# One Trainium2 core, attention and two expert layers: split steps asked for one by one, weight sums on Pool, decoding moved to the second batch

## The chip, the core and the metric

The program runs on one core of a Trainium2 chip. A time is the device time of one execution in microseconds. PE is the matrix engine, PEld its weight load, DVE the vector engine, ACT the scalar engine, POOL the GpSimd engine, and SP the engine whose queue issues every DMA of this kernel.

## What is computed

```python
# attention with decay: 2 batches, 8 heads, 768 steps, 64 wide
state = gamma * state + k_t v_t^T ;  y_t = scale * q_t state
# x: 1536 x 512. eight experts, every row through every expert, weighted by a balanced gate P
for e in range(8):
    h = np.maximum(x @ w1[e], 0.0)          # 512 -> 1024
    out += P[:, e:e + 1] * (h @ w2[e])      # 1024 -> 512
# last layer, 512 -> 2048 -> 512
h = x @ w_in
g = np.maximum(h, 0.0) + alpha * np.minimum(h, 0.0)
return g @ w_out
```

All is float32. `w_in` and `w_out` reach the core as 64-bit numbers and are turned into float32 there ("decoding").

## The kernel before

**Phases.** After the attention come 20 phases. Phases 0 to 7 are the eight experts on the first batch of 768 rows, phases 8 to 15 (`FAST`) the same experts on the second batch, and phases 16 to 19 the last layer, two halves of its 2048 columns for each batch. Each has a first layer (x times w1) and a second layer (h times w2).

**Products.** Every matrix is held as a high part (rounded by ACT) and a low part (what is left, by DVE or Pool), and a product takes three matmuls (`mm3`, L185 to L187). The first layer uses Strassen's scheme: each of four column blocks j has seven products p, so 28 products, in the order of the list `order`: place 0 is (0, 1), place 4 is (0, 7), place 7 is (0, 4), place 11 is (1, 7), place 14 is (1, 4), place 18 is (2, 7), place 21 is (2, 4), place 25 is (3, 7). The seven products of a block share PSUM banks. After product 1 ACT copies bank A to bank B (L687), product 6 adds to B, then DVE forms E = B + d (L690), product 7 adds to B, DVE forms D = B + d (L703; in phases 8 to 15 it writes b at L698), and product 4 adds to B. So PE can't start 6 before ACT's copy, 7 before DVE's E, or 4 before DVE's D.

**Second layers.** In phases 0 to 7 and 16 to 19 the second layer is plain, 6 row tiles of 8 products each; with each tile in two halves there are 12 slots, counted here as places 28 to 39. In phases 8 to 15 it is Strassen's scheme too, 28 units (places 28 to 55), whose right sides `hs` are split by ACT and DVE (L779, L780) and whose w2 pieces (`ws`) come from DRAM.

**Side work.** Four kinds of work ride on the phases, put after products by `at(ph, key, ...)`. (1) The w1 blocks of the next half phase: four adds (`w1_adds`, L113), then three parts a, c, b, each an ACT copy and a subtraction (`w1_part` through `split`, L97 and L98). The adds and lows of two blocks run on Pool, those of the other two on DVE in the second layer. (2) In phases 1 to 7, for the second batch, 32 tiles of w2 are prepared (`prep_load`, `prep_sums`, `prep_low`, `prep_store`): load 512 KB, four adds of 128x256 (L169) and directly behind them the ACT copy (L171), two lows of 128x512 (L175), two stores. Five of them go in each of phases 1 to 6. (3) 32 decodes (`decode_steps`): load, three DVE instructions (`bits`, L583 to L588), one on ACT, two on DVE (`join`, L599 and L602), store and next load. 17 lie in phases 1 to 6, one in phase 7 and 14 in phases 8 to 14. (4) The low parts of w2 (`w2_split`).

**What sets the order.** The schedule is written by hand: each engine's queue holds its instructions in the order in which the Python loop calls them, and an engine never passes over an instruction that waits. SP's queue holds all loads and stores the same way.

Of the kernel before, what the change touches and what calls it, by code (L numbers as in the profile page):

```python
# [44 lines left out]
def tile_kernel(ctx, tc, qkT, kv, ctab, w_gate, w1, w2, w_in, w_out, alpha, out):  # L45
# [235 lines left out]
    with tc.manual_schedule():  # L281
# [630 lines left out]

        xk = []
        for ph in range(len(PHASES)):
# [3 lines left out]
            for j in range(2):  # L918
                m = n + j + 2
                at(ph, (j, 1), lambda m=m: w1_adds(m, pool))  # L920
                at(ph, (j, 2), lambda m=m, eng=eng: w1_part(m, "a", eng))
                at(ph, (j, 7), lambda m=m, eng=eng: w1_part(m, "c", eng))
                at(ph, (j, 3), lambda m=m, eng=eng: w1_part(m, "b", eng))
# [197 lines left out]
```

## Time and profile before

| | us |
|---|---|
| median of 3 runs | 1392.34 (1390.39 to 1392.38) |
| the profiled execution | 1390.61 |
| its span in the profile | 1388.9 |
| PE busy | 1306.0 (94%) |
| DVE busy | 946.9 (68%) |
| ACT busy | 634.6 (46%) |
| Pool busy | 408.6 (29%) |

1.7 us lie outside the span. The page's slices show PE near full nearly everywhere and the granted clock at eight or nine tenths in slices of the first half. An engine's busy time is a sum over stages with different limits, so the stages are read one by one further down.

### The profile page before, as it was taken

What the parts mean: (1) busy time and instruction counts of PE and PEld (TensorE: products, weight loads), DVE (VectorE), ACT (ScalarE), POOL (GpSimd) and SP (SyncE); (2) the same over time, 40 slices, a digit from 0 to 9 for tenths busy, and PEclk for the clock granted to TensorE, in tenths of its full rate; (3) what the DMA queues carried; (4) which work ended last, traced back from release to release, by engine and by line L of the source; (5) the groups of instructions that cost most, each with busy time, mean ns of one, the idle gap of its engine ahead of it and who ended that gap; (6) DMA issues with size and microseconds to landing.
All of it is one profiled execution on the core that took longest, in us unless ns stands there. A gap on an engine that the chain in (4) does not pass through costs nothing.

```text
span 1388.9 us, 19473 instructions
## 1 busy us (share of the span) xinstructions
PE 1306.0 (94%) x7179; PEld 1208.2 (87%) x7179; DVE 946.9 (68%) x1562; ACT 634.6 (46%) x1129; POOL 408.6 (29%) x335
## 2 busy tenths in 40 slices
PE   9899898989797979879999999999999999999998
PEld 6798877778787868868899999999999998989897
DVE  5656676767776767675678786777877676486462
ACT  2553525243433334244546455464644546455360
POOL 4761414141323222230001312203121254426260
PEclk9999999989998999999999999999999999999999
DMA  9563687969696978785586776858577393052211
GB/s 364 174 212 125 198 280 236 315 201 316 216 322 201 319 232 299 252 273 185 195 284 194 271 217 227 297 172 287 183 274 231 112 351 107 31 159 84 77 31 46
DMA packets 152254, 296.80 MB, mean 214 GB/s; under 512 B 11952, under 2 KB 77024, under 8 KB 152160
## 3 DMA queue, kind: packets, MB, share of 16 engines
q1 hardware_dynamic: 152160, 295.57, 64.2%
q8 instruction: 56, 0.92, 0.3%
q14 instruction: 38, 0.31, 0.1%
HBM read 198.24 MB, written 97.28 MB: 213 GB/s over the span
## 4 chain that ended last, share of the span: by engine, by line
PE 66%; DVE 18%; ACT 6%; DMA 5%; issue 3%; SPq 2%; POOL 1%; ACTq 0%; DVEq 0%
PE B L185 8%; PE B L187 7%; PE B L186 7%; PE o L185 5%; PE o L187 5%; PE o L186 5%; PE A L185 4%; PE A L187 4%; PE A L186 4%; DVE pr L169 3%; DVE pr L175 3%; PE E L185 2%; PE E L186 2%; PE E L187 2%; PE D L187 2%
## 5 line engine op out<-in xcount | busy, mean ns | idle before, releaser
L113 POOL TENSOR_TENSOR raw<-raw 128x256 f32<-128x256 f32 x108 | 90.1, 845 | 207.3 <-DMA raw<-in_w_dram 62.5
L780 DVE TENSOR_TENSOR hs<-b,hs 128x768 fp32r<-128x768 f32 x96 | 95.0, 990 | 30.3 <-ACT hs L779 30.3
L690 DVE TENSOR_TENSOR E<-B,d 128x384 f32<-128x384 f32 x80 | 45.0, 563 | 80.8 <-PE B L187 75.5
L171 ACT ACTIVATE pw<-pr 128x1024 fp32r<-128x1024 f32 x32 | 33.9, 1060 | 141.0 <-DVE pr L169 136.0
L779 ACT ACTIVATE hs<-b 128x768 fp32r<-128x768 f32 x96 | 81.0, 844 | 28.9 <-PE B L187 10.7
L812 POOL TENSOR_TENSOR total<-total,t 128x384 f32<-128x384 f32 x56 | 60.0, 1100 | 105.2 <-DVE t L808 105.2
L687 ACT ACTIVATE B<-A 128x384 f32<-128x384 f32 x80 | 38.6, 482 | 87.6 <-PE A L187 85.9
L169 DVE TENSOR_TENSOR pr<-pr 128x256 f32<-128x256 f32 x128 | 65.8, 514 | 3.3
L249 POOL TENSOR_TENSOR xs<-b,xs 128x384 fp32r<-128x384 f32 x6 | 6.1, 1022 | 199.8 <-ACT xs L245 199.8
L187 PE MATMUL B<-hs,ws 128*128 128x384 f32 x192 | 64.2, 334 | 0.0
L185 PE MATMUL B<-hs,ws 128*128 128x384 f32 x192 | 64.2, 334 | 0.0
L186 PE MATMUL B<-hs,ws 128*128 128x384 f32 x192 | 64.2, 334 | 0.0
L175 DVE TENSOR_TENSOR pr<-pr,pw 128x512 fp32r<-128x512 f32 x64 | 48.7, 803 | 16.9 <-ACT pw L171 16.9
L738 DVE SCALAR_TENSOR_TENSOR total<-o,P,total 128x512 f32<-128x512 f32 x42 | 31.3, 746 | 28.9 <-PE o L187 28.9
L703 DVE TENSOR_TENSOR D<-B,d 128x384 f32<-128x384 f32 x48 | 27.0, 563 | 29.6 <-PE B L187 29.4
L113 DVE TENSOR_TENSOR raw<-raw 128x256 f32<-128x256 f32 x84 | 42.2, 519 | 1.4
L185 PE MATMUL A<-hs,ws 128*128 128x384 f32 x128 | 42.9, 335 | 0.0
L186 PE MATMUL A<-hs,ws 128*128 128x384 f32 x128 | 42.9, 335 | 0.0
L187 PE MATMUL A<-hs,ws 128*128 128x384 f32 x128 | 42.8, 335 | 0.0
L732 ACT ACTIVATE total<-o 128x512 f32<-128x512 f32 x18 | 10.8, 598 | 69.3 <-PE o L187 69.3
L645 ACT ACTIVATE hh<-D 128x384 fp32r<-128x384 f32 x32 | 15.7, 490 | 49.3 <-DVE D L703 49.3
L682 ACT ACTIVATE d<-D 128x384 f32<-128x384 f32 x64 | 31.1, 486 | 15.0 <-PE D L187 14.9
(3435 smaller groups left out, 4712.8 us busy)
## 6 DMA issues: line engine op xcount, KB each, us to landing
ws<-c SPq DMA_DIRECT2D x112, 512.0 KB, 5.7
raw<-in_w_dram SPq DMA_DIRECT2D x64, 512.0 KB, 4.7
c<-raw SPq DMA_DIRECT2D x32, 512.0 KB, 5.1
pr<-in_w_dram SPq DMA_DIRECT2D x32, 512.0 KB, 6.7
c<-pw SPq DMA_DIRECT2D x32, 512.0 KB, 5.3
c<-pr SPq DMA_DIRECT2D x32, 512.0 KB, 6.2
raw<-c SPq DMA_DIRECT2D x32, 512.0 KB, 5.4
raw<-wd SPq DMA_DIRECT2D x32, 512.0 KB, 3.6
```

The lines of the kernel that those rows point to most:

```text
L113: eng.tensor_tensor(out=out, in0=in0, in1=in1, op=op)
L169: nc.vector.tensor_tensor(out=out, in0=in0, in1=in1, op=op)
L171: nc.scalar.activation(out=ph2[i], in_=pr[i], func=AF.Copy)
L175: nc.vector.tensor_tensor(out=pr[i][:, a].bitcast(F32R), in0=pr[i][:, a], in1=ph2[i][:, a].bitcast(F32), op=ALU.subtract)
L185: nc.tensor.matmul(ps, ah, bh, start=first, stop=False, skip_group_check=True)
L186: nc.tensor.matmul(ps, ah, bl, start=False, stop=False, skip_group_check=True)
L187: nc.tensor.matmul(ps, alo, bh, start=False, stop=last, skip_group_check=True)
L687: nc.scalar.activation(out=banks[n, "B"], in_=banks[n, "A"], func=AF.Copy)
L690: nc.vector.tensor_tensor(out=banks[n, "E"], in0=banks[n, "B"], in1=banks[n, "d"], op=add)
L779: nc.scalar.activation(out=hi, in_=src, func=AF.Copy)
L780: nc.vector.tensor_tensor(out=lo, in0=src, in1=hi.bitcast(F32), op=ALU.subtract)
L812: nc.gpsimd.tensor_tensor(out=dst, in0=dst, in1=tt[m, h], op=ALU.add)
```

## The change

Every step of the side work gets its own place. `w1_part` falls into `w1_high` (the ACT copy) and `w1_low`, `prep_sums` into two halves and a separate `prep_high`, `hsplit` into `hhigh` and `hlow`. The four adds of the tiles that are prepared in a second layer go to Pool. In phases 1 to 6 the decode in the first layer is gone (12 decodes stay, all in second layers); phase 7 has none; phases 9 to 14 have three each, where they had two, the third in the second layer. A part of the diff (the lines that only rename or renumber are left out):

```diff
-    def w1_part(n, part, eng):
+    def w1_high(n, part):
...
-        hi, lo = split(wp, "w" + part, f"w{part}{n}", src, eng, width)
+        hi, lo = (wp.tile([128, width], F32R, tag=f"w{part}{w}", name=f"w{part}{n}{w}") for w in "hl")
+        nc.scalar.activation(out=hi, in_=src, func=AF.Copy)
+        ws1[n][part] = (lo, src, hi)
...
+    def w1_low(n, part, eng):
...
+        lo, src, hi = ws1[n].pop(part)
+        eng.tensor_tensor(out=lo, in0=src, in1=hi.bitcast(F32), op=ALU.subtract)
         if part == "b":
             w_load(0, n + 2)
...
-    def prep_sums(i):
+    def prep_sums(i, eng, part):
...
-        ):
-            nc.vector.tensor_tensor(out=out, in0=in0, in1=in1, op=op)
+        )[part]:
+            eng.tensor_tensor(out=out, in0=in0, in1=in1, op=op)
+
+    def prep_high(i):
         ph2[i] = pools["prep"].tile([128, 1024], F32R, tag="pw", bufs=2, name=f"pw{i}")
         nc.scalar.activation(out=ph2[i], in_=pr[i], func=AF.Copy)
...
+        def step(ph, pos, *fns):
+            for fn in fns:
+                key = order[pos] if pos < 28 else pos - 28 if ph in FAST else slots[pos - 28]
+                at(ph, key, fn)
...
-        def prep_at(ph, k1, k2, k3):
+        def prep_at(ph, eng, s0, s1, hi, lo, st):
...
-            at(ph, k1, lambda: prep_load(i + 1), lambda: prep_sums(i))
-            hooks.setdefault((ph, k2), []).insert(0, lambda: prep_low(i))
-            at(ph, k3, lambda: prep_store(i))
+            step(ph, s0, lambda: prep_load(i + 1), lambda: prep_sums(i, eng, slice(0, 2)))
+            step(ph, s1, lambda: prep_sums(i, eng, slice(2, 4)))
+            step(ph, hi, lambda: prep_high(i))
+            step(ph, lo, lambda: prep_low(i))
+            step(*(ph, st) if st < 40 else (ph + 1, st - 40), lambda: prep_store(i))
...
+            if 1 <= ph <= 6:
+                for i in (30, 36):
+                    decode_at(ph, i, i + 1, i + 2, i + 3)
+                prep_at(ph, dve, 5, 9, 13, 15, 19)
+                for q in (25, 30, 33, 36):
+                    h = max(q, 27)
+                    prep_at(ph, pool, q, q, h + 2, h + 3, h + 4)
+            elif ph == 7:
+                prep_at(ph, dve, 5, 9, 13, 15, 19)
+                prep_at(ph, dve, 18, 20, 22, 24, 26)
...
-            if 1 <= ph <= 6:
-                if ph > 1:
-                    decode_at(ph, *(order[i] for i in (10, 12, 14, 18)))
-                for i in (2, 8):
-                    decode_at(ph, *(slots[i + q] for q in (0, 1, 2, (4, 3)[i > 2])))
-                prep_at(ph, order[8], order[10], order[12])
-                for i in (0, 3, 6, 9):
-                    prep_at(ph, *slots[i:i + 3])
...
+                elif ph < 2 * E - 1:
+                    decode_at(ph, 4, 6, 7, 8)
+                    decode_at(ph, 12, 14, 15, 17)
+                    decode_at(ph, 40, 42, 43, 46)
```

Three places show what moves. The line numbers of after are higher by 14 to 18 for the same code (L181 are the prepared sums, L142 the w1 lows, L717 is D). The first place is DVE's queue in phase 4, first layer, from E of block 1 (after place 8) to D of block 1 (after place 11). Before:

```order
L690 TENSOR_TENSOR E_3598<-B_3567,d_3581 128x384
L646 SCALAR_TENSOR_TENSOR hl_10_3590<-B_3508,hh_10_3589 128x384
L169 TENSOR_TENSOR pr_3458<-pr_3458 128x256 x4
L646 SCALAR_TENSOR_TENSOR hl_01_3616<-E_3529,hh_01_3615 128x384
L175 TENSOR_TENSOR pr_3458<-pr_3458,pw_3607 128x512 x2
L583 TENSOR_SCALAR ex_0_0_3640<-rd_0_0_3497 128x512
L585 TENSOR_SCALAR a_0_0_3642<-rd_0_0_3497 128x512
L588 SCALAR_TENSOR_TENSOR a_0_0_3642<-rd_0_0_3497,a_0_0_3642 128x512
L703 TENSOR_TENSOR D_3574<-B_3567,d_3581 128x384
```

After:

```order
L181 TENSOR_TENSOR pr_3416<-pr_3416 128x256 x2
L704 TENSOR_TENSOR E_3580<-B_3540,d_3558 128x384
L660 SCALAR_TENSOR_TENSOR hl_10_3572<-B_3484,hh_10_3571 128x384
L181 TENSOR_TENSOR pr_3416<-pr_3416 128x256 x2
L660 SCALAR_TENSOR_TENSOR hl_01_3590<-E_3507,hh_01_3589 128x384
L717 TENSOR_TENSOR D_3551<-B_3540,d_3558 128x384
```

Two of the adds now stand ahead of E; the two lows and the three decode instructions have left the stretch. The lows now stand between E and D of block 2, the decode in the second layer. The second place is Pool's queue from the last w2 low of phase 4 into phase 5 (`raw` are the w1 adds). Before:

```order
L98 TENSOR_TENSOR v18l<-raw_18_3675,v18h 128x1024
L98 TENSOR_TENSOR v19l<-raw_19_3738,v19h 128x1024
L113 TENSOR_TENSOR raw_22_3956<-raw_22_3956 128x256 x4
L98 TENSOR_TENSOR wa22l<-raw_22_3956,wa22h 128x512
L98 TENSOR_TENSOR wc22l<-raw_22_3956,wc22h 128x768
L113 TENSOR_TENSOR raw_23_4055<-raw_23_4055 128x256 x4
```

After:

```order
L98 TENSOR_TENSOR v18l<-raw_18_3644,v18h 128x1024
L98 TENSOR_TENSOR v19l<-raw_19_3706,v19h 128x1024
L181 TENSOR_TENSOR pr_3543<-pr_3543 128x256 x4
L181 TENSOR_TENSOR pr_3808<-pr_3808 128x256 x4
L181 TENSOR_TENSOR pr_3895<-pr_3895 128x256 x4
L181 TENSOR_TENSOR pr_3967<-pr_3967 128x256 x4
L113 TENSOR_TENSOR raw_22_3947<-raw_22_3947 128x256 x4
L142 TENSOR_TENSOR wa22l<-raw_22_3947,wa22h 128x512
L113 TENSOR_TENSOR raw_23_4046<-raw_23_4046 128x256 x4
L142 TENSOR_TENSOR wc22l<-raw_22_3947,wc22h 128x768
```

Sixteen adds stand ahead of the w1 adds, and the second block's adds ahead of the first block's part c. The third place is DVE's queue in phase 10, second layer, behind E of the second half (place 39; `t` are the weighted results). Before:

```order
L841 TENSOR_TENSOR E_10_1_7719<-B_10_1_7633,d_10_1_7675 128x384
L98 TENSOR_TENSOR wc44l<-raw_44_7405,wc44h 128x768
L775 SCALAR_TENSOR_TENSOR hs_10_7733<-b_10_7336,hs_10_7733 128x768
L808 TENSOR_TENSOR t_00_7751<-A_10_0_7594,pb_7297 128x384
L98 TENSOR_TENSOR wb44l<-raw_44_7405,wb44h 128x512
L775 SCALAR_TENSOR_TENSOR hs_11_7760<-b_10_7503,hs_11_7760 128x768
L808 TENSOR_TENSOR t_10_7771<-A_10_1_7604,pb_7297 128x384
```

After:

```order
L859 TENSOR_TENSOR E_10_1_7664<-B_10_1_7578,d_10_1_7620 128x384
L597 TENSOR_SCALAR ex_5_1_7677<-rd_5_1_7442 128x512
L599 TENSOR_SCALAR a_5_1_7679<-rd_5_1_7442 128x512
L602 SCALAR_TENSOR_TENSOR a_5_1_7679<-rd_5_1_7442,a_5_1_7679 128x512
L794 SCALAR_TENSOR_TENSOR hs_10_7682<-b_10_7284,hs_10_7682 128x768
L142 TENSOR_TENSOR wc44l<-raw_44_7350,wc44h 128x768
L826 TENSOR_TENSOR t_00_7701<-A_10_0_7539,pb_7242 128x384
L794 SCALAR_TENSOR_TENSOR hs_11_7707<-b_10_7453,hs_11_7707 128x768
L826 TENSOR_TENSOR t_10_7718<-A_10_1_7549,pb_7242 128x384
L613 SCALAR_TENSOR_TENSOR a_5_1_7679<-a_5_1_7679,ex_5_1_7677 128x512
L616 SCALAR_TENSOR_TENSOR a_5_1_7679<-rd_5_1_7442,a_5_1_7679 128x512
```

The five DVE instructions of a third decode stand in a stretch that had none.

## Rows read from the trace of the kernel before

**Rows 1.** Windows, first layers, phases 1 to 7: length, busy PE, PEld, DVE, ACT, POOL; PEclk.
```profile
129.30:165.20 35.90, 31.71 (x173) 30.83 (x172) 19.28 (x32) 22.85 (x43) 17.02 (x12) 0.95 0.56 179
...
570.10:615.80 45.70, 33.80 (x170) 31.96 (x170) 34.33 (x55) 21.65 (x38) 17.99 (x12) 0.89 0.74 253
sum 291.80, PE 232.45 PEld 223.49 DVE 195.49 ACT 145.74 POOL 116.20; mean PE 33.21 PEld 31.93 DVE 27.93 ACT 20.82 POOL 16.60
```

**Rows 2.** Windows: first layer of phase 16, second of 4, first of 8; then DMA share.
```profile
1132.90:1162.70 29.80, 29.75 (x170) 29.17 (x170) 20.55 (x38) 21.68 (x40) 26.35 (x22) 1.00 0.63 222
388.00:420.50 32.50, 32.50 (x145) 26.89 (x145) 25.39 (x47) 8.49 (x13) 5.14 (x5) 1.00 0.96 313
649.60:685.70 36.10, 32.96 (x185) 32.18 (x184) 21.68 (x33) 19.14 (x36) 0.00 (x0) 0.95 0.64 213
```

**Rows 3.** Windows, phases 9 to 14, sums of six: first layers, then second layers.
```profile
sum 185.80, PE 177.74 PEld 175.80 DVE 130.59 ACT 104.50 POOL 35.56; mean PE 29.62 PEld 29.30 DVE 21.76 ACT 17.42 POOL 5.93
...
sum 173.80, PE 173.80 PEld 173.80 DVE 148.68 ACT 86.20 POOL 42.38; mean PE 28.97 PEld 28.97 DVE 24.78 ACT 14.37 POOL 7.06
```

**Rows 4.** Waits of PE, whole span: waiter, released by: us in total, times, longest.
```profile
PE B L185 <- DVE D L703: 40.3, 8, 5.8
PE B L185 <- ACT B L687: 16.3, 7, 3.8
PE B L185 <- DVE E L690: 13.3, 10, 3.1
```

**Rows 5.** Timeline, phase 4, around place 14: start, us, engine, line, shape [idle before <-releaser].
```profile
359.77 3.34 POOL L113 TENSOR_TENSOR raw<-raw 128x256 f32<-128x256 f32 x4
361.22 2.63 DVE L169 TENSOR_TENSOR pr<-pr 128x256 f32<-128x256 f32 x4
...
365.88 2.35 DVE L175 TENSOR_TENSOR pr<-pr,pw 128x512 fp32r<-128x512 f32 x2
...
368.15 1.48 DVE L583 TENSOR_SCALAR ex<-rd 128x512 uint32<-128x512 uint32 x1
...
370.61 0.56 DVE L703 TENSOR_TENSOR D<-B,d 128x384 f32<-128x384 f32 x1
...
371.23 0.69 PE L185 MATMUL B<-xh,wb17h 128*128 128x384 f32 x1 [5.83 <-DVE D L703]
```

**Rows 6.** Timeline, end of phase 4 and start of phase 5.
```profile
421.64 1.79 DVE L169 TENSOR_TENSOR pr<-pr 128x256 f32<-128x256 f32 x4
...
423.51 1.06 ACT L171 ACTIVATE pw<-pr 128x1024 fp32r<-128x1024 f32 x1 [2.70 <-DVE pr L169]
...
425.00 0.44 PE L185 MATMUL B<-xh,wc20h 128*128 128x384 f32 x1 [2.29 <-ACT B L687]
```

**Rows 7.** Groups of instructions: count, then busy us, mean ns, idle us before.
```profile
L113 POOL TENSOR_TENSOR raw<-raw 128x256 f32<-128x256 f32 x108 | 90.1, 845 | 207.3 <-DMA raw<-in_w_dram 62.5 <-DVE raw L113 55.1 <-DMA raw<-wd 39.1
...
L169 DVE TENSOR_TENSOR pr<-pr 128x256 f32<-128x256 f32 x128 | 65.8, 514 | 3.3
L175 DVE TENSOR_TENSOR pr<-pr,pw 128x512 fp32r<-128x512 f32 x64 | 48.7, 803 | 16.9 <-ACT pw L171 16.9
...
L599 DVE SCALAR_TENSOR_TENSOR a<-a,ex 128x512 f32<-128x512 f32 x32 | 25.2, 787 | 1.0 <-DVE a L588 0.5
```

**Rows 8.** Window of the whole span, instructions on tile rd alone: DVE busy.
```profile
0.00:1388.90 1388.90, 74.94 (x128) 0.98 0.64 214
```

**Rows 9.** Timeline of DVE, phase 4, between D of block 1 and D of block 2.
```profile
373.81 1.61 DVE L98 TENSOR_TENSOR v16l<-raw,v16h 128x1024 fp32r<-128x1024 f32 x1 [1.52 <-ACT v16h L97]
...
379.73 0.56 DVE L703 TENSOR_TENSOR D<-B,d 128x384 f32<-128x384 f32 x1
```

**Rows 10.** Timeline of DVE, phase 10, second layer, near its end.
```profile
828.35 1.77 DVE L780 TENSOR_TENSOR hs<-b,hs 128x768 fp32r<-128x768 f32 x1
830.04 0.54 DVE L805 TENSOR_TENSOR t<-B,d 128x384 f32<-128x384 f32 x1
```

**Rows 11.** DMA issues: size, median us from issue to landing.
```profile
pr<-in_w_dram SPq DMA_DIRECT2D x32, 512.0 KB, 6.7
```

More of the change, by code (lines that the diff above doesn't have):

```diff
@@ L917, in tile_kernel @@
             eng = dve if fast else pool
[L918 to L923, printed above, removed]
-            if not fast:
+            if 1 <= ph <= 6:
[8 more added lines that the diff above has]
+                prep_at(ph, dve, 18, 20, 22, 24, 26)
+            if fast:
+                w1_at(ph, n + 2, pool, dve, 0, 2, 3, 3, 5, 7, 9)
+                w1_at(ph, n + 3, pool, dve, 5, 9, 10, 10, 12, 14, 16)
+                w1_at(ph, n + 4, pool, dve, 36, 36, 38, 39, 41, 42, 44)
+                w1_at(ph, n + 5, pool, dve, 44, 44, 46, 47, 49, 50, 52)
+            else:
+                w1_at(ph, n + 2, pool, pool, 0, 3, 3, 6, 6, 9, 9)
+                w1_at(ph, n + 3, pool, pool, 5, 10, 10, 12, 12, 16, 16)
+                if ph > 0:
+                    w1_at(ph, n + 4, dve, dve, 29, 29, 30, 31, 32, 31, 32)
+                    w1_at(ph, n + 5, dve, dve, 33, 33, 34, 35, 36, 35, 36)
                 for j, key in enumerate(((2, 1), (2, 2), (3, 1), (2, 3))):
@@ L967, in tile_kernel @@
-                for key, jp in ((5, 0), (7, 1)):
-                    at(ph, key, lambda ph=ph, jp=jp: t4(ph, jp))
+                        step(ph, (1, 4, 6, 8)[q // 2], lambda m=q // 2, h=q % 2: gather(m, h))
+                step(ph, 0, lambda ph=ph: weight_load(ph))
+                for pos, fn, jp in ((17, t1, 0), (20, t2, 0), (24, t3, 0), (27, t1, 1), (29, t2, 1), (31, t3, 1)):
+                    step(ph, pos, lambda ph=ph, fn=fn, jp=jp: fn(ph, jp))
+                highs = (11, 25, 18, 28, 21, 30, 32, 34, 36, 38, 40, 42, 44, 46)
@@ L969, in tile_kernel @@
+                lows = (13, 26, 19, 28, 23, 30, 32, 34, 36, 38, 40, 42, 44, 46)
+                for k in range(14):
+                    step(ph, highs[k], lambda ph=ph, k=k: hhigh(ph, k))
+                    step(ph, lows[k], lambda ph=ph, k=k: hlow(ph, k))
+                for pos, jp in ((33, 0), (35, 1)):
+                    step(ph, pos, lambda ph=ph, jp=jp: t4(ph, jp))
                 if ph in (E + 1, E + 4):
-                    at(ph, (0, 1), lambda k=(ph - E - 1) // 3: xk.extend(x_keep(2, k)))
+                    step(ph, 0, lambda k=(ph - E - 1) // 3: xk.extend(x_keep(2, k)))
@@ L971, in tile_kernel @@
                 if E < ph < 2 * E - 1:
-                    for keys in (((2, 1), (2, 2), (2, 7), (3, 4)), (9, 11, 13, 17), (18, 20, 22, 27)):
+                    for keys in ((12, 17, 18, 27), (37, 39, 41, 45), (46, 48, 50, 55)):
                         i = unit[0] - NJ * E
@@ L976, in tile_kernel @@
                         unit[0] += 1
-                        for q, key in enumerate(keys):
-                            at(ph, key, lambda i=i, q=q: xk[i][q]())
+                        for q, pos in enumerate(keys):
+                            step(ph, pos, lambda i=i, q=q: xk[i][q]())
             if ph + 1 in XGROUP:
@@ L1040, in tile_kernel @@
             for t in range(TT):
[L1041 to L1042 removed]
+                do(ph, f"t{t}a")
                 do(ph, f"t{t}")
```

77 lines of the change are left out of this document (31 added, 46 removed).

## The prediction

> **What bounds the kernel now.** I read the windows by stage first, then PE's waits, then the timelines around the longest of them. Phase 16 shows what a first layer takes when nothing is late: 29.8 us, PE busy for 29.75 of them, granted clock 1.00 [rows 2]. The same 28 products take 291.8 us in the seven phases 1 to 7 [rows 1], where 7 x 29.8 = 208.6 would do: 83.2 us over. PE's busy sum there is 232.45, so 59.3 us are idle, and the other 24 are matmuls at a lower clock (0.95 in phase 1, 0.89 in phase 7). The second layers have nothing to give: PE is busy for 32.50 of 32.50 us [rows 2]. Phase 8 is 36.1 - 29.8 = 6.3 over [rows 2], and the first layers of phases 9 to 14 are 185.8 - 6 x 29.8 = 7.0 over [rows 3]. So 83.2 + 6.3 + 7.0 = 96.5 us is all that side work can give back.
>
> Who ends these waits: DVE's D 40.3 us in 8 waits, ACT's copy to B 16.3 in 7, DVE's E 13.3 in 10 [rows 4]. The reader should see queues here, not slow engines. Before the D that frees product 4 of block 1, DVE works off the adds of a w2 tile (2.63 us, stretched beside Pool's adds), its lows (2.35) and three decode instructions (the first 1.48); D comes at 370.61, PE has been idle for 5.83 us, and its next matmul shows 0.69 us [rows 5]: the clock has fallen to the lower of its two levels, 1.2 GHz. At a phase's start ACT's copy of a w2 tile waits 2.70 us for DVE's adds, the copy to B stands behind it, and PE is idle for 2.29 us [rows 6].
>
> **The change part by part.** A product takes 29.8/28 = 1.06 us, a second-layer slot 32.5/12 = 2.71 us [rows 2].
>
> The wait at place 14. PE gives DVE five products, 5.3 us, from the end of product 6 (place 8) to the start of product 4 (place 14). DVE now has E, two hl and D in that stretch, taken at D's 0.56 each [rows 5], and two adds, 1.0 us at the mean of 0.514 [rows 7] or 1.3 at the pace of rows 5: 3.3 to 3.6 us. It fits, so the 5.8 us and the fall of the clock go.
>
> What is late next: D of block 2, behind the lows that came there. D to D took 379.73 - 370.61 = 9.12 us [rows 5, 9], 1.52 of it a wait for ACT. A decode costs DVE 74.94/32 = 2.34 us on its loaded tile [rows 8] and 0.79 for the fifth instruction [rows 7], 3.13 together; its two last, some 1.4, leave this stretch and two lows, 1.6 us at the mean [rows 7], 2.35 at worst [rows 5], come in: 9.3 to 10.1, with D itself 9.9 to 10.6. PE gives nine products, 9.6 us. I expect a wait of 0.4 us a phase; the bounds are below 0 (the 1.52 us can take up the lows) and 1.0.
>
> The wait at the phase's start. `prep_high` stands two slots, 5.4 us, behind Pool's four adds, 3.4 us at 0.845 [rows 7]; ACT need not wait for them, and the 16.3 us of rows 4 go. The last low of a phase stands just ahead of the next phase's E. DVE's second layer is 25.39 us busy [rows 2]; without 16 adds of 0.514, 8.2 us, it is 17.2. Pool's 16 adds are 13.5 us. If every one of them held DVE for its whole length, DVE would need 30.7 of 32.5 us. So it ends in time on the whole; I put 0.5 us on its lateness at the end (0 to 1.5) and 0.6 on waits that today's longer ones hide. That is 1.5 us of waits a phase, 31.3 us for a first layer, none long enough for the clock to fall. In phase 7 a second tile stays on DVE in the first layer, four adds and two lows, 2.1 + 1.6 = 3.7 us more late in it: 3.0 us of waits (1.5 to 5.2), 32.8. Together 6 x 31.3 + 32.8 = 220.6, and 291.8 - 220.6 = **71.2 us gained**.
>
> Pool itself: the adds are 0.845 us here against 0.514 on DVE, 1.64 times [rows 7]. The Trainium skill ("GPSIMD Engine Reference", Engine selection) speaks against the move: two-input elementwise work belongs on VectorE, GpSimd being about two times slower; the trace agrees in direction, and by its factor of two the 16 adds would be 16.4 us instead of 13.5, which Pool also has room for. Pool is busy for 5.14 us of the second layer [rows 2] and 16.6 of the first [rows 1]; with 13.5 it has 18.6 of 32.5. Behind its new adds stand the w1 adds and lows of the next phase, and ACT's w1 copies and PE wait for those. The cover: a tile's load lands 6.7 us after issue [rows 11], three slots are 8.1, and PE first uses these weights at place 12, 12.7 us into the phase. If the cover goes, each us of lateness is a us of PE.
>
> SP's queue holds the same loads and stores; a tile's stores come about one slot later, and a store that waits for its low holds the loads behind it. The DMA share is 0.96 in the second layer [rows 2] and keeps its four tiles and two decodes; the first layer (0.56 to 0.74 [rows 1]) loses a decode but is shorter. I cost it at nothing, with the load's 6.7 us as cover.
>
> Phases 9 to 14. The first layers' 7.0 us of waits behind DVE's E go: the w1 copies are asked for before the ACT work that they stood behind. The third decode goes into second layers where DVE is busy for 24.78 of 28.97 us [rows 3]; 3.13 more make 27.9. In phase 10 the add at 830.04 ends at 830.58 [rows 10], and unit 25, product 4 of the second half, starts at 806.1 + 25 x 1.036 = 832.0: 1.4 us to spare against 3.1, so up to 1.7 us late. Less if DVE is less held by Pool, as in the 1.77 us split of rows 10. I take 0.7 a phase, 4.2, and net **2.8 gained** (between 7.0 - 10.2 = -3.2 and 7.0).
>
> Phase 8 keeps its decodes; its last w1 copy is asked for two products earlier, so that loads and stores behind it leave earlier: **2.0 gained** of 6.3 (0 to 6.3). Phases 0 and 16 to 19 only change slots where PE is already full: nothing, within 1.
>
> Sum: 71.2 + 2.8 + 2.0 = 76.0, and 1390.6 - 76.0 = 1314.6. The profiled execution lay 0.2 us above the fastest and 1.7 below the median, so the forecast is **1315 us**, its own range 1302 to 1325.
>
> **The rivals.** A: Pool's adds hold DVE. For it: DVE's four adds took 2.63 us beside Pool's [rows 5] and 1.79 elsewhere [rows 6]. Pool now adds all through the second layer, so DVE enters the next phase late, or the lows meet Pool's w1 lows, and PE waits some 3 us a phase in one go. Rows 6 show 2.29 us with the clock down after it; the lower clock costs 24.2/7 = 3.5 us a phase now, for two falls, so 1.75 for one. 4.75 instead of 1.5 is 3.25 more, times 7 is 23: 1338. Against it: the 30.7 of 32.5 above. The Trainium skill ("SBUF — State Buffer", Who interferes with whom) states the rule behind it: a DVE instruction with two SBUF inputs and a GpSimd instruction that reads SBUF exclude each other, and the later one blocks fully until the other ends. The stretched adds of rows 5 agree.
>
> B: the second batch gives back more. All of the 1.7 us in six second layers (10.2 instead of 4.2), and the second decode, whose load is now asked for four products before its use instead of seven, 4.2 us where loads of its size take 6.7 [rows 11], holds E of block 2 and eats the 7.0: 6 + 7 = 13, 1328. For it: DVE is the fullest engine beside PE there. Against it: PE has two products to spare at that E.
>
> C, slower than before: Pool becomes the bound of phases 1 to 7. Its work there is 16.6 + 5.1 + 13.5 = 35.2 us, a phase is 41.7 + 32.5 = 74.2 now. From 2.1 times today's pace on, under the exclusion from DVE, the phases grow; at 2.3 times it is 81 us, 6.8 x 7 = 48 more: 1438. Against it: the 0.845 us of rows 7 already stand beside a busy DVE.
>
> D: the waits only move, to D of block 2 or E, and no time changes: 1388 to 1393. It needs 10 us of new waits a phase, where DVE has 27.93 - 3.13 = 24.8 us of work in a first layer of 29.8.
>
> E: no wait is left: 1390.6 - 96.5 = 1294, up to 1301.
>
> **How the numbers follow.** Chances: forecast 0.55, A 0.20, B 0.14, E 0.06, C 0.03, D 0.02. The range from 1300 to 1342 takes in forecast, A and B and leaves out E, C, D and the tails. About 0.2% is what a measurement of this kernel can tell from no change; faster by more holds for all but C and D: 0.95, same 0.02, slower 0.03.
>
> **What would show it.** Right: no wait for ACT's copy to B over 1 us in phases 1 to 7, no wait for D at place 14, granted clock 1.00 throughout these phases, first layers of 30 to 32 us, second layers still 32.5 with DVE at some 20 to 25 us and Pool at 18 or more. For A: a wait for E at place 4 or D at place 21 of 2 us and more, with a lower clock behind it. For B: second layers of phases 9 to 14 over 29.0 us with a PE wait for DVE's t. For C: PE waiting at places 12 to 19 for Pool's w1 lows. The forecast is wrong if the first layers of phases 2 to 6 stay above 35 us.

## The result, and the profile after

The changed kernel took 1338.04 us (median of four runs, 1336.02 to 1340.08) against 1391.37 of the kernel before in the same comparison; the ratio is 0.962, 95% interval 0.9598 to 0.9642. It is faster, and inside the stated range of 1300 to 1342; but it lies outside the forecast's own range of 1302 to 1325, 23 us above the forecast of 1315. The profiled execution took 1338.82 us with a span of 1336.8, 52.1 less than before.

Windows of the changed kernel, columns as in [rows 1] (PEclk and DMA share near the end): the sum of the first layers of phases 1 to 7, the second layer of phase 4, the first layer of 8, and of phases 9 to 14 the sums of first and of second layers.

```profile
sum 224.80, PE 210.31 PEld 204.44 DVE 165.78 ACT 133.33 POOL 130.25; mean PE 30.04 PEld 29.21 DVE 23.68 ACT 19.05 POOL 18.61
...
353.00:385.50 32.50, 32.50 (x145) 26.91 (x144) 25.21 (x37) 9.62 (x13) 17.55 (x18) 1.00 0.92 310
...
581.30:619.40 38.10, 33.52 (x185) 32.55 (x184) 21.94 (x33) 18.92 (x37) 0.00 (x0) 0.91 0.64 209
...
sum 192.30, PE 182.00 PEld 178.76 DVE 141.57 ACT 105.60 POOL 44.39; mean PE 30.33 PEld 29.79 DVE 23.59 ACT 17.60 POOL 7.40
...
sum 181.50, PE 176.04 PEld 173.58 DVE 164.69 ACT 89.54 POOL 34.38; mean PE 29.34 PEld 28.93 DVE 27.45 ACT 14.92 POOL 5.73
```

| stage | before | after | change | predicted |
|---|---|---|---|---|
| first layers, phases 1 to 7 | 291.8 [rows 1] | 224.8 | -67.0 | -71.2 |
| first layer, phase 8 | 36.1 [rows 2] | 38.1 | +2.0 | -2.0 |
| first layers, phases 9 to 14 | 185.8 [rows 3] | 192.3 | +6.5 | -7.0 |
| second layers, phases 9 to 14 | 173.8 [rows 3] | 181.5 | +7.7 | +4.2 |
| before phase 0 | 63.74 | 62.37 | -1.4 | 0 |

The sum is -52.2. The other stages moved by half a us or less, phases 16 to 19 taken together; within them single stages moved by up to 1.8 us either way (the first layer of phase 18 took 31.5 us instead of 29.7, with a wait of 1.6 for D, the second layer of phase 17 32.8 instead of 34.5). The attention before phase 0 has the same code and took 62.4 to 65.0 in the runs below, so that row is scatter. PE's waits in the changed kernel, as in [rows 4]:

```profile
PE B L199 <- DVE D L717: 11.2, 9, 1.6
PE B L199 <- DVE E L704: 10.5, 11, 4.1
PE B L199 <- DVE b L712: 9.1, 7, 2.0
PE B L199 <- DVE t L823: 4.8, 4, 1.2
...
PE B L199 <- ACT B L701: 0.8, 4, 0.2
```

The long D waits and ACT's copy to B are gone. Two lines are new: b (product 7 of phases 8 to 15) and t (the result add of their second layers).

**What is left in phases 1 to 7**: some 2.0 us a phase, as in phase 4. DVE's timeline there (start, us, engine, line, shape, idle before), with PE's late product 4 of block 2:

```profile
331.73 2.93 DVE L181 TENSOR_TENSOR pr<-pr 128x256 f32<-128x256 f32 x2
...
335.05 0.55 DVE L717 TENSOR_TENSOR D<-B,d 128x384 f32<-128x384 f32 x1
...
338.25 2.03 DVE L98 TENSOR_TENSOR v16l<-raw,v16h 128x1024 fp32r<-128x1024 f32 x1 [1.53 <-ACT v16h L97]
340.20 0.55 DVE L704 TENSOR_TENSOR E<-B,d 128x384 f32<-128x384 f32 x1
340.81 0.44 PE L199 MATMUL B<-xh,wc18h 128*128 128x384 f32 x1 [0.71 <-DVE E L704]
...
341.13 2.22 DVE L189 TENSOR_TENSOR pr<-pr,pw 128x512 fp32r<-128x512 f32 x2
...
345.48 0.45 PE L199 MATMUL B<-xh,wb18h 128*128 128x384 f32 x1 [1.28 <-DVE D L717]
```

The two adds ahead of D took 2.93 us, beside Pool's w1 lows, which follow one another from 331.10 to 335.8. So D of block 1 came 1.2 us after PE had finished product 7 (place 11, at 333.8). PE had enough in hand there, but the delay runs on through ACT, whose copies stand behind that D and for which DVE then waits 1.53 us, into E and D of block 2, where PE waits 0.71 and 1.28 us.

**Phase 9**, first layer: DVE and Pool ahead of b, and PE behind it.

```profile
663.74 0.43 DVE L597 TENSOR_SCALAR ex<-rd 128x512 uint32<-128x512 uint32 x1 [0.95 <-DMA rd<-in_w_out_dram]
...
666.11 0.63 ACT L133 ACTIVATE wb39h<-raw 128x512 fp32r<-128x512 f32 x1 [1.41 <-PE E L200]
...
668.65 1.03 POOL L263 TENSOR_TENSOR xs<-b,xs 128x384 fp32r<-128x384 f32 x1 [118.06 <-ACT xs L259]
669.66 1.44 POOL L255 TENSOR_TENSOR ta<-b 128x384 f32<-128x384 f32 x1
...
667.39 0.69 DVE L613 SCALAR_TENSOR_TENSOR a<-a,ex 128x512 f32<-128x512 f32 x1 [0.81 <-ACT ex L607]
668.12 0.69 DVE L616 SCALAR_TENSOR_TENSOR a<-rd,a 128x512 uint32<-128x512 uint32 x1
668.73 1.51 DVE L142 TENSOR_TENSOR wb39l<-raw,wb39h 128x512 fp32r<-128x512 f32 x1
670.16 1.74 DVE L768 TENSOR_TENSOR b<-b,b 128x768 f32<-128x768 f32 x1
...
672.43 0.44 PE L199 MATMUL B<-xh,wb38h 128*128 128x384 f32 x1 [2.02 <-DVE b L712]
```

Between E (place 15) and b (place 18) DVE now has the end of the second decode, which waits 0.81 us for ACT's `ex`, then a w1 low and t1, these two stretched by Pool's x pieces. ACT's `ex` (666.65) stands behind a w1 copy that waits 1.41 us for PE. In the kernel before, the low and t1 stood ahead of b too, behind the first instructions of a decode, and were done before Pool began:

```profile
733.65 0.69 DVE L98 TENSOR_TENSOR wb39l<-raw,wb39h 128x512 fp32r<-128x512 f32 x1
734.25 0.95 DVE L754 TENSOR_TENSOR b<-b,b 128x768 f32<-128x768 f32 x1
...
735.29 1.02 POOL L249 TENSOR_TENSOR xs<-b,xs 128x384 fp32r<-128x384 f32 x1 [119.53 <-ACT xs L245]
```

**Phase 8**: DVE, PE, and SP's queue (each `xd<-tt` stores a turned block).

```profile
610.57 0.43 DVE L599 TENSOR_SCALAR a<-rd 128x512 uint32<-128x512 uint32 x1 [5.34 <-DMA xd<-tt]
...
613.12 0.69 PE L199 MATMUL B<-xh,wc35h 128*128 128x384 f32 x1 [4.12 <-DVE E L704]
...
603.14 0.38 SPq L896 DMA_DIRECT2D xd<-tt  x1
```

DVE's `a` needs a buffer of the tag that the turned blocks use too, and waits 5.34 us for the last store to land. That store leaves 21.8 us into the phase; before it was 22.1 (671.68 - 649.6). The earlier w1 copy moved it by 0.3 us only. DVE's `a` begins 7.4 us behind that store's issue, where it was 6.5 before; PE waits 4.12 us for E instead of 3.08, and the granted clock of the stage is 0.91 instead of 0.95 [rows 2]. Why the store lands later was not followed up.

### The profile page after: what moved, and what is told of

It reads as the page before. It is cut to its first block, busy times and chain, and to the rows that moved or that the text cites. A ratio compares the mean times of both kernels' runs of the same rounds, so it can differ in the third digit from the quotient of the medians.

```text
span 1336.8 us, 19524 instructions
## 1 busy us (share of the span) xinstructions
PE 1289.4 (96%) x7179; PEld 1192.1 (89%) x7179; DVE 946.7 (71%) x1466; ACT 637.4 (48%) x1129; POOL 501.4 (38%) x431
## 4 chain that ended last, share of the span: by engine, by line
PE 69%; DVE 13%; DMA 6%; ACT 4%; issue 4%; POOL 2%; SPq 2%; ACTq 0%; DVEq 0%; POOLq 0%
PE o L199 8%; PE o L201 8%; PE o L200 8%; PE B L199 6%; PE B L201 6%; PE B L200 6%; PE A L199 4%; PE A L201 4%; PE A L200 4%; PE D L201 2%; PE D L200 2%; PE D L199 2%; PE E L199 2%; PE E L200 2%; PE E L201 2%
## 5 line engine op out<-in xcount | busy, mean ns | idle before, releaser
L181 POOL TENSOR_TENSOR pr<-pr 128x256 f32<-128x256 f32 x96 | 92.6, 964 | 89.8 <-DMA pr<-in_w_dram 33.6
L788 ACT ACTIVATE hs<-b 128x768 fp32r<-128x768 f32 x112 | 94.5, 844 | 44.7 <-DVE b L768 20.4
L798 DVE TENSOR_TENSOR hs<-b,hs 128x768 fp32r<-128x768 f32 x96 | 98.5, 1026 | 24.0 <-ACT hs L788 23.9
L830 POOL TENSOR_TENSOR total<-total,t 128x384 f32<-128x384 f32 x56 | 63.7, 1168 | 119.8 <-DVE t L826 119.8
L263 POOL TENSOR_TENSOR xs<-b,xs 128x384 fp32r<-128x384 f32 x6 | 7.4, 1226 | 188.0 <-ACT xs L259 188.0
L189 DVE TENSOR_TENSOR pr<-pr,pw 128x512 fp32r<-128x512 f32 x64 | 62.8, 1020 | 0.0
L717 DVE TENSOR_TENSOR D<-B,d 128x384 f32<-128x384 f32 x48 | 26.9, 561 | 27.8 <-PE B L201 27.8
L199 PEld LDWEIGHTS B<-hs,ws 128*128 128x128 f32 x192 | 36.0, 188 | 7.9 <-DVE t L823 6.1
L607 ACT ACTIVATE ex<-ex,ebias 128x512 uint32<-128x512 uint32 x32 | 23.1, 721 | 40.4 <-DVE ex L597 40.4
```

Source lines behind the costliest of these rows:

```text
L181: eng.tensor_tensor(out=out, in0=in0, in1=in1, op=op)
L189: nc.vector.tensor_tensor(out=pr[i][:, a].bitcast(F32R), in0=pr[i][:, a], in1=ph2[i][:, a].bitcast(F32), op=ALU.subtract)
L199: nc.tensor.matmul(ps, ah, bh, start=first, stop=False, skip_group_check=True)
L788: nc.scalar.activation(out=t[:, 0, :], in_=hsource(ph, k), func=func)
L798: nc.vector.tensor_tensor(out=lo, in0=src, in1=hi.bitcast(F32), op=ALU.subtract)
L830: nc.gpsimd.tensor_tensor(out=dst, in0=dst, in1=tt[m, h], op=ALU.add)
```

## The experiments

Stage sums below are read from phase boundaries as in the table above. Phases 9 to 14 with unchanged code gave first layers of 188.6 to 192.3 in sum, with zero to two falls of the clock after b, so less than 4 us there says nothing. The changed kernel's own profile is the longest of them: by these runs the change costs these first layers 2.8 to 6.5 us, not 6.5.

### What gave the 67 us back

**The adds on DVE again**

```diff
-                    prep_at(ph, pool, q, q, h + 2, h + 3, h + 4)
+                    prep_at(ph, dve, q, q, h + 2, h + 3, h + 4)
```

> The changed kernel with the sixteen adds per phase of the second layers of phases 1 to 6 back on DVE, at the same places. Theory 'places' (what counts is where a step stands in a queue, not which engine adds): DVE was busy for 25.2 of 32.5 us in the second layer of phase 4 with the adds on Pool and 25.4 in the kernel before with them on DVE, so the move bought DVE nothing; ACT's copy still stands two slots behind the adds. 1334 to 1345 us, no wait for ACT's copy to B. Rival 'Pool' (the move took the wait at the phase's start away): that wait, 16.3 us in all before, and the lower clock behind it come back, 1358 to 1366.

Measured: 1339.49 us, ratio to before 0.9641 (0.9625 to 0.9657). First layers of phases 1 to 7: 225.2 against 224.9. The second layer of phase 4 here:

```profile
355.70:388.20 32.50, 32.50 (x145) 26.90 (x144) 28.71 (x54) 9.86 (x13) 3.51 (x5) 1.00 0.91 309
```

The move to Pool is worth nothing that these runs can tell from scatter. Pool's 14.0 us more (17.55 against 3.51) bought DVE 3.5 us (25.21 against 28.71), not 8.2, and DVE had no need of these 3.5.

**Adds on DVE and the copy directly behind them, as before**

```diff
-                for q in (25, 30, 33, 36):
-                    h = max(q, 27)
-                    prep_at(ph, pool, q, q, h + 2, h + 3, h + 4)
+                for q in (28, 31, 34, 37):
+                    prep_at(ph, dve, q, q, q, q + 1, q + 2)
```

> The changed kernel with the second layers of phases 1 to 6 asking for their tiles as the kernel before did: adds on DVE in slots 0, 3, 6, 9, ACT's copy directly behind them, lows one slot and stores two slots later. Theory 'places': ACT's copy of the last tile holds the copy to B at the start of phases 2 to 7, some 2.3 us each with 1.75 at the lower clock: six times 4 is 24, 1362 us (1355 to 1368). Rival 'decode' (the decode's leaving the first layer is what gave the time, since DVE enters the phase earlier): at most 4 us over the changed kernel, 1336 to 1342.

Measured: 1342.55 us, 0.9676 (0.9645 to 0.9706); first layers of phases 1 to 7 +3.9 us, ACT's copy to B 3.9 us in all. The theory fell: with the decodes where the change has them, the copy's place is worth 3.9 us, not 24.

**The decode back in the first batch**

```diff
+            if 2 <= ph <= 7:
+                decode_at(ph, 10, 12, 14, 18)
...
-                    decode_at(ph, 40, 42, 43, 46)
```

> The changed kernel with six decodes back in the first layers of phases 2 to 7, at the kernel before's places 10, 12, 14, 18, and none in the second layers of phases 9 to 14. Theory 'DVE's stretch to D': the three first instructions, 1.5 us, stand between E and D of block 1 where some 0.4 us are to spare, the two last, 1.4 us, before D of block 2, which is 1.3 us late already: 2.5 us of new waits and one or two falls of the clock, 4.5 to 6 us in each of six phases, 27 to 36, less 7.6 us in the second layers of phases 9 to 14 (back to 29.0 each): 1357 to 1366. Rival 'lows alone' (moving the prepared lows out of the stretch did it, the decode fits): first layers stay under 33 us, 1330 to 1336.

Measured: 1360.32 us, 0.9791 (0.9776 to 0.9807): first layers of phases 1 to 7 +32.8, second layers of phases 9 to 14 -7.6, to 173.9. As the theory had it in size; but the larger wait is at E of block 2 (up to 3.8 us), and D of block 1 is waited for 1.3 to 1.8 us. DVE before that E:

```profile
352.88 2.03 DVE L98 TENSOR_TENSOR v16l<-raw,v16h 128x1024 fp32r<-128x1024 f32 x1 [2.14 <-ACT v16h L97]
...
355.55 1.79 DVE L616 SCALAR_TENSOR_TENSOR a<-rd,a 128x512 uint32<-128x512 uint32 x1
...
357.87 0.69 PE L199 MATMUL B<-xh,wc18h 128*128 128x384 f32 x1 [3.75 <-DVE E L704]
```

**The first layer's tile in one piece, as before** (phases 1 to 6)

```diff
-                prep_at(ph, dve, 5, 9, 13, 15, 19)
+                prep_at(ph, dve, 8, 8, 8, 10, 12)
```

> The changed kernel with the first layer's tile in phases 1 to 6 asked for as in the kernel before: four adds and the copy at place 8, lows at 10, stores at 12 (the decode stays out). Theory 'queue before D': adds 2.63, lows 2.35, two hl and D, 1.7, are 6.7 us where PE gives 5.3: 1.4 us of wait and here and there a fall of the clock, less the 1.3 us at D of block 2: 0 to 2.5 us a phase, 1338 to 1353. Rival 'halves add up' (putting the decode back cost 33 us in the first layers, so the split of the tile is the other 34): 1365 to 1373.

Measured: 1356.21 us, 0.9758 (0.9723 to 0.9794); first layers of phases 1 to 7 +19.5, all in phases 1 to 6, with D of block 1 waited for 3.1 to 3.9 us:

```profile
342.48 2.45 DVE L181 TENSOR_TENSOR pr<-pr 128x256 f32<-128x256 f32 x4
346.48 0.56 DVE L660 SCALAR_TENSOR_TENSOR hl<-E,hh 128x384 fp32r<-128x384 f32 x1 [1.55 <-ACT hh L659]
346.96 2.35 DVE L189 TENSOR_TENSOR pr<-pr,pw 128x512 fp32r<-128x512 f32 x2
349.23 0.55 DVE L717 TENSOR_TENSOR D<-B,d 128x384 f32<-128x384 f32 x1
...
345.02 1.06 ACT L185 ACTIVATE pw<-pr 128x1024 fp32r<-128x1024 f32 x1 [4.01 <-issue]
345.98 0.47 ACT L659 ACTIVATE hh<-E 128x384 fp32r<-128x384 f32 x1
```

3 us above the theory's upper end: it counted DVE's instructions, not the 1.55 us in which DVE waits for ACT, whose `hh` stands behind the copy that waited for DVE's adds. The rival's 34 us did not come either.

**The decode moved, alone, in the kernel before**

```diff
-                if ph > 1:
-                    decode_at(ph, *(order[i] for i in (10, 12, 14, 18)))
...
+                if ph > E:
+                    decode_at(ph, 12, 14, 15, 18)
```

(phase 7's decode is out too.)

> The kernel before with one part of the change alone: the six decodes leave the first layers of phases 2 to 7, phases 9 to 14 get a third in the second layer (units 12, 14, 15, 18); all other places, DVE's adds and ACT's copies stay as they were. Theory 'queue': the wait for D of block 1 falls from 5.8 us to the 3.1 to 3.9 that the first layer's tile makes when it is asked for in one piece, ACT's copy to B at a phase's start shrinks to 1 us or less as it did when the copies stood behind their sums without the decode, and the wait for E at block 2 that a decode put back made (3.7 us) goes: first layers of phases 2 to 6 at 34 to 37, 30 to 38 us gained there, some 5 lost in phases 9 to 14: 1357 to 1366. Rival 'additive': the other edits are needed for the start of a phase, its 16.3 us of waits and the lower clock stay, 1372 to 1382.

Measured: 1378.07 us, 0.9918 (0.989 to 0.9947): first layers of phases 1 to 7 -17.6, second layers of phases 9 to 14 +6.4. The rival held: ACT's copy to B is still waited for, 15.2 us in all. The trace shows what it waits for, at the end of phase 3: SP's queue, DVE and ACT up to the next phase's first products.

```profile
322.74 0.44 SPq L159 DMA_DIRECT2D pr<-in_w_dram  x1
...
326.23 3.05 DVE L113 TENSOR_TENSOR raw<-raw 128x256 f32<-128x256 f32 x4
...
329.30 0.33 SPq L124 DMA_DIRECT2D c<-raw  x1
...
331.11 1.29 SPq L607 DMA_DIRECT2D wd<-a  x1
332.45 1.20 SPq L573 DMA_DIRECT2D rd<-in_w_in_dram  x1
...
339.43 0.43 DVE L583 TENSOR_SCALAR ex<-rd 128x512 uint32<-128x512 uint32 x1 [3.36 <-DMA rd<-in_w_in_dram]
...
343.37 1.06 ACT L171 ACTIVATE pw<-pr 128x1024 fp32r<-128x1024 f32 x1 [2.69 <-DVE pr L169]
344.34 0.47 ACT L687 ACTIVATE B<-A 128x384 f32<-128x384 f32 x1
...
344.86 0.59 PE L185 MATMUL B<-xh,wc16h 128*128 128x384 f32 x1 [3.10 <-ACT B L687]
```

SP stands from 323.2 to 329.3 before the store of a w1 block (`c<-raw`), which waits for DVE's w1 adds. The second decode's load stands behind it, leaves at 332.45 and lands at 339.4; DVE waits 3.36 us, and the last tile's adds, its copy and the copy to B follow late. The change turns that order round: its first decode is stored at place 33 instead of 34 and asked for ahead of the w1 work, so that the decode's store and load stand ahead of `c<-raw`. The prediction had passed over that. The kernel before shows the same wait at the end of phase 4, just ahead of the late adds of [rows 6]; there the load left at 412.87, behind a `c<-raw` at 409.28:

```profile
419.56 0.43 DVE L583 TENSOR_SCALAR ex<-rd 128x512 uint32<-128x512 uint32 x1 [2.54 <-DMA rd<-in_w_out_dram]
```

**That load ahead, in the same kernel**

```diff
-                    decode_at(ph, *(slots[i + q] for q in (0, 1, 2, (4, 3)[i > 2])))
+                    decode_at(ph, *(slots[i + q] for q in (0, 1, 2, (2, 3)[i > 2])))
```

> The kernel before with the decodes moved (as in the run before it of that kind), and one step more: in the second layers of phases 1 to 6 the first decode's store, and with it the load for the second, is asked for in slot 4 instead of 6, so that on SP both stand ahead of the store of the w1 block (c1), which waits for DVE's w1 adds. Theory 'load': the 2.3 to 3.1 us wait for ACT's copy to B at the start of phases 2 to 7 comes from that load, issued some 7 us before the phase's end and held behind that store; DVE waited 3.4 us for it, and the last tile's adds, ACT's copy of it and the copy to B came after. Issued some 8 us earlier, the wait shrinks to 1.3 us or less and the clock stays up at the start: 3 to 4 us in each of six phases, 1353 to 1361. Rival 'amount': the last tile's adds and copy are late anyway by DVE's and the DMA's load in the second layer, the waits for ACT stay over 2 us, 1373 to 1380.

Measured: 1361.2 us, 0.979 (0.9765 to 0.9814): first layers of phases 1 to 7 another -13.8, the wait for ACT's copy 1.3 us in all (15.2), DVE's `ex` without a wait:

```profile
321.77 0.43 SPq L573 DMA_DIRECT2D rd<-in_w_in_dram  x1
324.62 0.33 SPq L124 DMA_DIRECT2D c<-raw  x1
...
331.85 0.42 DVE L583 TENSOR_SCALAR ex<-rd 128x512 uint32<-128x512 uint32 x1
```

So the theory holds, at the edge of its range: one load's place in SP's queue is 14 us here. Of the 17 in all, 1.2 came in phase 8 and 1.6 in phases 16 to 19, which is not claimed for it.

### Where the rest was lost

**Lows of the first layer's tile behind D of block 2** (phases 1 to 6)

```diff
-                prep_at(ph, dve, 5, 9, 13, 15, 19)
+                prep_at(ph, dve, 5, 9, 13, 19, 23)
```

> The changed kernel with the two lows of the first layer's tile in phases 1 to 6 asked for at place 19 instead of 15, behind D of block 2 (stores at 23 instead of 19). Theory: the 1.3 us wait for D of block 2 is these lows, 2.22 us beside Pool, and goes: 6 x 1.3 = 8, 1330 us, first layers 30.6. Rival: D of block 3 or the next phase's first E is late instead, first layers stay at 31.9, 1336 to 1340.

Measured: 1334.26 us, 0.9602 (0.9582 to 0.9622), between the two. The waits for D fall from 11.2 to 3.9 us; first layers of phases 1 to 6 are 30.4 to 31.5; phase 7, whose own steps the edit leaves alone, took 34.5 instead of 33.1: -4.7 together. Its rival came in part: in phases 2, 3, 4, 6 and 7 PE now waits 0.6 to 1.4 us for the phase's first E (place 4), where the changed kernel has one such wait, 0.70 us in phase 2.

**Turned blocks in other buffers** (the tag `pu`, which no decode uses)

```diff
-            t = tp.tile([128, HT], F32, tag="tmp", name=f"tt{g}_{a}{h}")
+            t = tp.tile([128, S], F32, tag="pu", bufs=2, name=f"tt{g}_{a}{h}")[:, 0:HT]
```

> The changed kernel with the turned blocks of phases 7 and 8 in buffers of their own instead of the two that the decodes' ex and a use. Theory: the 4.1 us wait for E in phase 8 and the fall of the clock behind it come from DVE's a, which waited 5.3 us for the store of a turned block to land: the wait goes, first layer of phase 8 from 38.0 to 30 to 31 us, 1331 us. Rival: the decode's own load or the stores behind it hold DVE just as long, first layer 36 us or more, 1336 to 1340.

Measured: 1332.68 us, 0.9596 (0.9562 to 0.963); phase 8's first layer 31.9 (38.0), its wait for E gone, a wait for b of 0.85 us left. The shared buffers cost 6 us here. The kernel before has the same wait (DVE's `a`, 3.33 us for `xd<-tt`); it was not run without it.

**The third decode elsewhere**

```diff
             elif ph == 7:
+                for i in (30, 36):
+                    decode_at(ph, i, i + 1, i + 2, i + 3)
...
-                    decode_at(ph, 40, 42, 43, 46)
+                    if ph in (11, 14):
+                        decode_at(ph, 40, 42, 43, 46)
+                else:
+                    decode_at(ph, 4, 6, 7, 8)
+                    decode_at(ph, 12, 14, 15, 17)
```

> The changed kernel with the third decode taken out of phases 9, 10, 12 and 13 (it stays in 11 and 14); two decodes more stand in phase 7's second layer and two in phase 15's first. Theory 'third decode': it alone makes DVE late for the result add in those four second layers, which go back from 30.9 to 29.0, 7.6 us, and the added ones cost nothing: 1331 us. Rival 'Pool': these four are the phases in which Pool prepares three x pieces and not one, and DVE's split and lows beside it hold the add anyway: second layers stay at 30 to 31, 1336 to 1340.

Measured: 1332.14 us, 0.9589 (0.9551 to 0.9627). Second layers of phases 9 to 14 173.9, no wait for t: as the theory had it. Phases 8 and 15 lost 3.6 us (phase 8 starts with 0.9 us of waiting for ACT, phase 15 waits 1.0 for b).

**A w1 low and t1 behind b**

```diff
-                w1_at(ph, n + 3, pool, dve, 5, 9, 10, 10, 12, 14, 16)
+                w1_at(ph, n + 3, pool, dve, 5, 9, 10, 10, 12, 14, 19)
...
-                for pos, fn, jp in ((17, t1, 0), (20, t2, 0), ...
+                for pos, fn, jp in ((18, t1, 0), (20, t2, 0), ...
```

> The changed kernel with two steps of phases 8 to 15 moved behind product 7 of block 2: the low of part b from place 16 to 19 and t1 from 17 to 18. Theory: the waits for b before place 21, 8.6 us over phases 9 to 14, are these two instructions, 1.5 and 1.7 us beside Pool's adds, ahead of b in DVE's queue: they go, and so do the falls of the clock in phases 9 and 12: first layers of phases 9 to 14 from 192 to 182 to 185 us, 1329 to 1332. Rival 'amount' (DVE has a decode too many there): the wait turns up at E of block 2 or 3, sum 189 or more, 1335 to 1340.

Measured: 1327.87 us, 0.9555 (0.9522 to 0.9587). First layers of phases 9 to 14 182.7 (192.3, and 188.6 at least in the other runs), no wait for b there; E and ACT's copy are waited for 0.2 to 0.8 us at a time in phases 10 to 14. The queue theory holds, except that what stretches the two is Pool's x pieces, not its adds. DVE's wait for the second decode's load is still there (1.61 us in phase 9). Phase 8, whose steps move too, took 34.5 and 30.2 (38.0 and 29.0).

**The four together, and one step more**

The four edits above, with the taken decodes at other places and the second tile of phase 7 later:

```diff
             elif ph == 7:
+                decode_at(ph, 30, 31, 32, 33)
-                prep_at(ph, dve, 5, 9, 13, 15, 19)
-                prep_at(ph, dve, 18, 20, 22, 24, 26)
+                prep_at(ph, dve, 5, 9, 13, 19, 23)
+                prep_at(ph, dve, 20, 22, 24, 27, 29)
...
+                else:
+                    decode_at(ph, 4, 6, 7, 8)
+                    decode_at(ph, 12, 14, 15, 17)
+                    decode_at(ph, 40, 42, 43, 46)
```

> The changed kernel with the four repairs together: lows of the first layer's tile behind D of block 2 in phases 1 to 7, own buffers for the turned blocks, no third decode in phases 9, 10, 12 and 13 (one more in phase 7's second layer, three in phase 15), low of part b and t1 behind b; the second tile of phase 7 two places later. If the repairs add up: first layers of phases 1 to 7 218 (-7), phase 8 at 31 (-7), phases 9 to 14 183 and 174 (-9.5 and -7.6): 1307 us. If they collide (DVE late for E of block 3, or phase 15 too full): 1315 or more.

Measured: 1317.6 us, 0.948 (0.9456 to 0.9504): 10 us above the 1307 that was said for the case that they add up. What the four single runs measured adds up to some 1313 by their medians and to 0.948 by their ratios, so the total does not tell whether they collide; the stages do. Phases 9 to 14 are at 180.2 and 173.9; the first layers of phases 1 to 7 gave 1.3 us only (phase 7 34.5; the phase's first E, at place 4, waited for 1.4 us in phases 2, 5 and 6), where the lows alone gave 4.7, and phase 8 is at 33.6 with a wait for b of 2.3, where the buffers alone gave 31.9. So in these stages the repairs collide. In phase 7 E of block 3 is late by 2.5 us: DVE waits 3.28 us for ACT's `d`, which stands behind a w2 copy that waits 4.02 us for its load. In phase 8, as in the run before this one, DVE waits 1.05 us for ACT's `ex` and has the decode's end, a split and t3 ahead of b. The step more:

```diff
-                    at(ph, key, lambda m=n + j, eng=dve if j < 2 and 0 < ph < E else pool: w2_split(m, eng))
+                    at(ph, key, lambda m=n + j, eng=dve if j == 1 and 0 < ph < E else pool: w2_split(m, eng))
```

> As the run with the four repairs, and in phases 1 to 7 the low of the first w2 tile, 2.03 us on DVE ahead of E of block 2, on Pool. Theory: the 0.7 us wait for E at place 18 is this low, and goes: 4 to 5 us under the run with the four repairs. Rival: Pool's next low is later by 2.4 us and DVE is held more beside it, within 2 us of that run or above it.

Measured: 1314.78 us, 0.9468 (0.9445 to 0.9491), against 0.948 without the step: the intervals overlap. By stage, first layers of phases 1 to 7 are 3.1 us shorter (220.4), between theory and rival. E of block 2 is waited for nowhere in them; but the run without the step has that wait in phase 1 alone (0.72 us), so there was little for the low to give. What is left in phases 2 to 6 is a wait of 0.7 to 1.6 us for the phase's first E. This version is ahead of both kernels, of the changed one by some 1.6% going by the ratios.

## Why the prediction was right and where it failed

**Phases 1 to 7, -67.0 for -71.2.** Right in size, and by most marks: no wait for ACT's copy to B over 1 us, none at place 14, clock 1.00, first layers of 31.8 to 33.1 (30 to 32 was said), second layers of phases 1 to 6 at 32.5. Two marks missed a little: there Pool is busy for 16.2 to 18.9 us, where 18 or more was said, and DVE for 24.1 to 25.9, where 20 to 25 was said; the sum had it at 17.2, and the adds' leaving freed 3.5 us in place of 8.2. Its reading of place 14 holds for the tile, which costs 19.5 us in one piece, at that place. It holds in part for the decode: put back it costs 32.8 us, but more of that at E of block 2 (up to 3.8 us a phase) than at place 14 (1.3 to 1.8). The step on the phase's start failed in its cause. It gave that wait to the place of `prep_high` and let Pool's adds free DVE; these two together are worth 3.9 us, the adds alone nothing (225.2 against 224.9). What the runs show in its place is the decode's load behind `c<-raw`, 13.8 us by the last run on it. Whether the later copy alone would have done it, with that load still late, was not run. The prediction costed SP's queue "at nothing" with the 6.7 us of a load as cover, and never asked what held DVE before the late adds of rows 6.

The missing 4 us are the step "what is late next": 0.4 us for D of block 2, "bounds below 0 and 1.0". It took DVE to begin at D of block 1 as soon as PE allowed, with two adds of 1.0 to 1.3 us ahead; they took 2.93 beside Pool's lows, D of block 1 was 1.2 us late without a wait to show for it, and the debt came due at E and D of block 2: 2.0 us. The term of 0.5 us for a late DVE at place 4 was nothing but in phase 2.

What the parts are worth does not add up to 67 by simple sums. The kernel before with the decode moved and the load ahead stands at 260.2 in these stages, the changed kernel at 224.9. Of the 35.3 between them the tile in pieces is 19.5 in phases 1 to 6, phase 7 is 7.9 (41.0 and 33.1) and the copies and their places 3.9; 4 us stay unassigned.

**Phase 8, +2.0 for -2.0.** The step "its last w1 copy is asked for two products earlier" moved the store by 0.3 us. It didn't follow the stall to its end, a buffer that two unrelated tiles share; taking that away gives 6.1. Why the stall grew by a us stays open.

**Phases 9 to 14, +14.2 for -2.8.** This is rival B, in both its places, while the forecast took the small end. In the second layer up to 1.7 us late was named and 0.7 taken; it is 1.9 us each where it happens (30.9 against 29.0), in the four phases in which Pool prepares three x pieces and DVE's instructions are the longest. In the first layer (+2.8 to +6.5) B had the right decode and, for the larger part, the wrong cause. Its later load (5.0 to 6.0 us to landing by its own rows; the 6.7 of [rows 11] is another load's) is indeed waited for by DVE, 0.95 to 2.31 us in each of the six phases, and PE waits 0.7 us for E of block 2 in two of them. But b waits without it too: with the decode back in the first batch, the load of phase 14 was there in time, and PE still waited 1.22 us for b, behind this:

```profile
1003.39 0.69 DVE L613 SCALAR_TENSOR_TENSOR a<-a,ex 128x512 f32<-128x512 f32 x1 [1.50 <-ACT ex L607]
```

The decode's end waits for ACT, so a low and t1, which always stood ahead of b, now fall beside Pool's x pieces; moving these two behind b took the wait away. The clock fell behind b in two phases (granted 0.95 in phases 9 and 12). The forecast looked for what the edit removes (waits for E of block 3, which went) and not for what now stands in front of the next release.

**Rival A's 1338 is a coincidence.** The 23 us above the forecast are 17.0 from phases 9 to 14, 4.2 from phases 1 to 7 and 4.0 from phase 8, less 1.4 of scatter ahead of phase 0. A's marks, a wait of 2 us and more with the clock down in phases 1 to 7, are not there, and taking Pool's adds away changes nothing. (That the clock falls behind the wait of [rows 6] does not stand in the row given, a matmul of 0.44 us; it shows at 425.71, where one takes 0.52.) C and D are out; E is not reached by the best version either.

## To carry to other kernels

When a wait goes, list what stands in the queue ahead of the next two releases, with the stretched durations and with the delay that was hidden so far: a debt that costs nothing at one release is paid at the next. Follow a late DVE instruction back through the DMA that it waits for to the queue that issued it: here a load behind a store that waited for compute was late by that compute, and asking for it ahead of the store cost nothing. Undo each part of a change that does five things; here the one that the title names (Pool) was worth nothing, and one that the diff hardly shows, 14 us.
